# Gated linear attention and a cosine-gated layer on one Trainium2 core: where the weights' checks, the weights' halves and the log sums stand in the loop over groups

## The chip, the cores and the metric

The kernel runs on one core of one Trainium2 chip. The metric is device time in microseconds (us). Three runs of the kernel before gave 665.95, 669.12 and 670.2; their median is 669.12. One execution was recorded by the hardware profiler; every duration below is from it.

## The reference, cut to what matters

```python
# q, k, v, a_re, a_im: (B=4, H=8, S=768, D=48)
mag = np.sqrt(a_re * a_re + a_im * a_im)
scale = np.minimum(mag, 0.999) / (mag + 1e-06)
a_re_n, a_im_n = (a_re * scale, a_im * scale)
for t in range(S):
    ar, ai = (a_re_n[:, :, t, :, None], a_im_n[:, :, t, :, None])
    new_re = ar * S_re - ai * S_im
    new_im = ar * S_im + ai * S_re
    kv = np.einsum('bhd,bhe->bhde', k[:, :, t], v[:, :, t])
    S_re, S_im = (new_re + kv, new_im)
    y[:, :, t] = np.einsum('bhd,bhde->bhe', q[:, :, t], S_re)
x = y.transpose(0, 2, 1, 3).reshape(B * S, H * D)      # 3072 x 384
h = x @ w_in                                           # 384 x 2048
g = h * np.cos(h)
out = g @ w_out                                        # 2048 x 384
```

The state decays by a complex gate at each step; only its real part is read. The two weights arrive as 8-byte floats.

## The kernel before

**Chunks and groups.** The 768 steps of a batch are cut into chunks of 128 (24 chunks in all); two chunks make a group, so there are 12 groups, three to a batch. Within a chunk the recurrence is turned into products: a sum over time of the logs of the gates' magnitudes and a sum of their phases give, through exponentials and cosines, factors for the queries and keys; scores (`sc`, queries by keys, masked by VectorE into `atm`), value products (`yp`) and state sums (`sp`) follow on TensorE (PE). The group's result goes to memory as x and comes back turned as xT, two DMAs (L1066, L1075). Then come the group's hidden sums x @ w_in (`hp`, tiles jp = 0 to 7, each of 256 columns of w_in in two halves of 128 rows), the gate h*cos(h) (a sine with a shift of half pi on ScalarE (ACT), a check `junk`/`wide` on the size of h, a product on VectorE (DVE)), and the products with w_out, arranged as seven products of blocks of which the sums and differences (`s`, `t_s`, `t_a`, `gate` mixes) are made beforehand.

**Three-term tiles.** From group 3 on the tiles jp 4 and 5, from group 4 on also 6 and 7, are computed another way: the weight is cut into an upper part wh and a scaled rest wl (`halves`, L1099: three DVE instructions that make `cut`, wl and wx, then two ACT instructions that write wh and scale wl), and x into xh and xl (`x_halves`, L1116). PE then makes xh*wh + xl*wl (the straight part) and a cross sum `hb` from xx and wx.

**A software pipeline.** The loop `for n in range(2, NG)` (L1721) runs, for each n, attention of group n, the products of group n-1, the logs, keys and phases of group n+1 and the hidden sums of group n. `weave` (L1356) gives every list of steps a stretch of the interval 0 to 1 and writes the steps down in that order: attention and products fill the first half, `first(n)`, the eight hidden-sum tiles, stands from 0.56 to 1.0. A scheduler then orders each engine; `chain` fixes the order of PE, of ACT's table-based functions (`special`, L709, and `upper_half`, L726; the last of them is `tail["scalar"]`) and of SyncE's (SP's) DMAs; `behind(a, b)` puts a behind b on one engine. A last `weave` after the loop (L1738) does the products of group 11.

**Logs.** `log_steps` (L736 to L791) makes magnitude and angle of the gates of the next group; its last instruction is a Relu over `re` that adds up negative entries in `odd`. `upper_half` splits the logs into hi (ACT) and lo (DVE); `prods` (L1386) multiplies both by triangular ones on PE (`lgs`), and ACT takes the exponentials of it. The powers at a chunk's end leave through a small DMA called row (L843) and come back as `end` (L850). SP's queue carries, in the order of the program, row, the x and xT of the group, and at the group's end the turned keys and queries: two moves `moved<-tr` (L948), four `kT<-moved` (L951) and one `qT<-moved` (L953).

**Guards.** A check on the 8-byte weights rides along in the loop. `fetched` (L627) loads a piece of 768 KB by GpSimd's (POOL's) queue (L631) into a tile `raw`, which in the loop shares its one buffer (`tr`) with the turned keys and queries; `guard` (L647) takes the exponent from the upper words by a shift on DVE, and ACT's Relu of (897 - exponent) adds up what is too small, in place. `guarded` (L1425) first lets POOL wait for a named gate of group n-1. There are 16 pieces, two in each of the groups 4 to 11. POOL's wait stands at position 0.1; load and check of a group's first piece are written at 0.22, of its second at 0.93, the end of the hidden sums. The second load can go out when tr is free.

L691 is the line of every matmul, L680 that of nearly every DVE and ACT instruction that has no other helper, L711 that of the table functions, so what follows goes by tiles.

Of the kernel before, what the change touches and what calls it, by code (L numbers as in the profile page):

```python
# [11 lines left out]
F32 = mybir.dt.float32  # L12
# [475 lines left out]
def fast_path(ctx, tc, q, k, v, a_re, a_im, moe_w_in, moe_w_out, out, least, odd, wide,  # L488
# [46 lines left out]
    tail = {}  # L535
# [124 lines left out]
    least_e_b = scalar_tile(897.0, "least_e_b")  # L660
# [75 lines left out]
    def log_steps(g, i, n):  # L736
# [43 lines left out]
        if lower:  # L780
# [9 lines left out]
        scalar.activation(out=junk, in_=re, func=AF.Relu, scale=-1.0,  # L790
                          accum_out=odd[:, ds(next(odds), 1)])  # L791
# [307 lines left out]
    def halves(jp):  # L1099

        for name in "wl", "wx":
            if name not in right:
# [4 lines left out]
        vector.tensor_scalar(out=cut_.bitcast(U32), in0=w.bitcast(U32), scalar1=UPPER,  # L1107
                             scalar2=None, op0=ALU.bitwise_and)
# [4 lines left out]
        scalar.copy(out=w_in[jp], in_=cut_)  # L1113
        scalar.mul(out=wl, in_=wl.bitcast(F32), mul=SHIFT)

    def x_halves(g):  # L1116
# [14 lines left out]
        def lower():  # L1131
            behind(scalar.copy(out=x["xh"], in_=x["cut"]), x["square"])
# [3 lines left out]
            behind(low, x["product"])  # L1136

        def apart():
            behind(vector.scalar_tensor_tensor(
                out=x["xx"], in0=x["xl"].bitcast(F32), scalar=-SHIFT,  # L1140
                in1=x["cut"], op0=ALU.mult, op1=ALU.add), x["product"])
# [6 lines left out]
    def mm1_three(g, jp, ps):  # L1148
# [27 lines left out]
        for part in (straight, crossed) if "held" not in x else (crossed, straight):  # L1176
            part()
# [39 lines left out]
    def mm1(g, jp, last):  # L1217

        mm1_sums(g, jp)
        if three(g, jp):  # L1220
            cross_out(g, jp)
            if "held" in X[g]:
                mm1_gate(g, X[g]["held"])
# [4 lines left out]
        if last:  # L1228
# [3 lines left out]
            if "held" in X[g]:  # L1232
                mm1_gate(g, X[g]["held"])
# [191 lines left out]
    def guarded(g, count):  # L1425
# [3 lines left out]
        for _ in range(min(count, len(guards))):  # L1429
            yield lambda: guard(guards.pop(0), X[g + 1].get("product"))  # L1430
# [3 lines left out]
    per = -(-len(guards) // (NG - 4))  # L1434
# [399 lines left out]
```

## Time and profile before

| what | value |
|---|---|
| profiled execution, its own time | 670.13 us |
| its span in the trace | 668.2 us |
| PE matmul busy | 634.7 us, 95% |
| PE weight loads busy (beside matmuls) | 575.4 us, 86% |
| DVE busy | 528.7 us, 79% |
| ACT busy | 432.9 us, 65% |
| POOL busy | 31.2 us, 5% |
| chain that ended last | PE 70%, ACT 9%, DVE 8%, DMA 7% |

The span is the time from the first to the last recorded instruction; about 2 us of the execution lie around it. Busy shares are means over stages. A row of the timeline reads: start, duration, engine, line, operation, written tile<-read tiles, shape, count of instructions run together, and in brackets the idle time ahead of it and who ended it. For DMA issues the duration is the time on the issuing queue, not the transfer. A row of the windows reads: stretch and length, busy time (with instruction count) of PE, PE's weight loads, DVE, ACT and POOL, the granted clock of PE, the DMA engines' share and GB/s.

### The profile page before, as it was taken

The numbers are of one execution on the slowest core, as the hardware profiler recorded it, in microseconds if no ns is written. First come the engines' busy times: TensorE is split into PE (matmuls) and PEld (weight loads), VectorE is DVE, ScalarE is ACT, GpSimd is POOL, SyncE is SP. The second block draws the span as 40 slices with busy tenths as digits, with TensorE's granted clock in tenths as the row PEclk, the third lists the DMA queues.
The fourth block names the chain that finished last, engine by engine and source line by source line (L and its number), as shares of the span: only waits on it lengthen the run. The fifth ranks groups of instructions, "written<-read, shape, count | busy, mean of one in ns | idle before, by whom it ended". The sixth has DMA issues, their size and how long they took to land.

```text
span 668.2 us, 11342 instructions
## 1 busy us (share of the span) xinstructions
PE 634.7 (95%) x4279; PEld 575.4 (86%) x4279; DVE 528.7 (79%) x862; ACT 432.9 (65%) x787; POOL 31.2 (5%) x53
## 2 busy tenths in 40 slices
PE   8999989998899999989999999989989999999977
PEld 6888867766799899989989989989979999989977
DVE  6999989687598899788699799787779889873361
ACT  7898777372694794695695695596586586552440
POOL 4011100000000000000000000000000000000000
PEclk9999999999899999999999999998999999999999
DMA  9967855538417816936925926926844942544000
GB/s 237 258 189 170 250 142 152 120 71 218 89 26 165 237 25 137 256 82 127 270 78 119 270 75 132 272 71 123 231 108 84 278 110 52 173 88 142 24 2 29
DMA packets 232922, 94.93 MB, mean 142 GB/s; under 512 B 208701, under 2 KB 221246, under 8 KB 232858
## 3 DMA queue, kind: packets, MB, share of 16 engines
q1 hardware_dynamic: 225320, 68.51, 44.6%
q0 software_dynamic: 5824, 25.50, 11.4%
q8 instruction: 35, 0.57, 0.4%
q10 hardware_dynamic: 1714, 0.11, 0.2%
q14 instruction: 29, 0.24, 0.1%
HBM read 69.28 MB, written 24.81 MB: 141 GB/s over the span
## 4 chain that ended last, share of the span: by engine, by line
PE 70%; ACT 9%; DVE 8%; DMA 7%; issue 4%; SPq 1%; ACTq 0%; POOL 0%; POOLq 0%; DVEq 0%
PE hp L691 23%; PE op L691 14%; PE sum L691 14%; PE yp L691 5%; PE sc L691 4%; PE sp L691 3%; DMA qT<-moved 3%; PE phs L691 2%; PE hb L691 2%; ACT junk L680 2%; DVE hp L680 1%; ACT gate L711 1%; DMA xT<-x 1%; DVE gate L680 1%; PE lgs L691 1%
## 5 line engine op out<-in xcount | busy, mean ns | idle before, releaser
L691 PE MATMUL hp<-xT,w_in 128*128 128x256 f32 (+1 forms) x768 | 166.5, 376 | 7.1 <-DVE gate L680 5.1
L691 PEld LDWEIGHTS hp<-xT,w_in 128*128 128x128 f32 x768 | 143.0, 192 | 28.1 <-DVE gate L680 5.5
L711 ACT ACTIVATE gate<-hp,half_pi_b 128x512 f32<-128x512 f32 x96 | 65.9, 687 | 62.6 <-PE hp L691 45.7
L691 PE MATMUL op<-w_out,gate 128*128 128x192 f32 (+1 forms) x464 | 103.6, 373 | 1.2 <-DVE gate L680 1.2
L691 PEld LDWEIGHTS op<-w_out,gate 128*128 128x128 f32 x464 | 78.5, 190 | 18.7 <-issue 2.0
L680 DVE TENSOR_TENSOR gate<-hp,gate 128x512 f32<-128x512 f32 x62 | 42.5, 685 | 37.3 <-ACT junk L680 37.0
L680 ACT ACTIVATE ot<-sum 128x192 f32<-128x192 f32 x39 | 12.8, 328 | 72.3 <-PE sum L691 72.0
L691 PE MATMUL sc<-qT,kT 96*128 96x128 f32 x384 | 49.6, 277 | 10.5 <-DMA qT<-moved 7.8
L691 PEld LDWEIGHTS sc<-qT,kT 96*128 96x128 f32 x384 | 46.9, 192 | 13.4 <-issue 10.8
L680 ACT ACTIVATE junk<-hp 128x512 bf16<-128x512 f32 x96 | 56.7, 590 | 0.0
L691 PE MATMUL sum<-w_out,gate 128*128 128x192 f32 x304 | 54.6, 328 | 0.0
L691 PEld LDWEIGHTS sum<-w_out,gate 128*128 128x128 f32 x304 | 49.2, 190 | 0.0
L680 DVE SCALAR_TENSOR_TENSOR gate<-hp,gate 128x512 f32<-128x512 f32 x34 | 23.5, 691 | 25.9 <-ACT junk L680 25.9
L680 DVE TENSOR_TENSOR atm<-sc,causal 128x512 f32<-128x512 f32 x48 | 32.5, 684 | 8.6 <-PE sc L691 8.6
L691 PE MATMUL hp<-xh,wh 128*128 128x256 f32 x204 | 37.0, 290 | 0.0
L691 PE MATMUL hp<-xl,wl 128*128 128x256 f32 x204 | 35.2, 281 | 0.0
L691 PE MATMUL yp<-atm,v 128*48 128x128 f32 x352 | 34.2, 280 | 0.7 <-DVE atm L680 0.7
L691 PE MATMUL sum<-t_s,gate 128*128 128x192 f32 x160 | 31.7, 352 | 2.5 <-DVE gate L680 2.5
L680 DVE TENSOR_TENSOR gate<-gate 128x256 f32<-128x256 f32 x80 | 32.2, 419 | 1.9 <-PE op L691 1.3
L691 PEld LDWEIGHTS sum<-t_s,gate 128*128 128x128 f32 x160 | 27.4, 201 | 5.4 <-issue 4.4
L707 ACT ACT_TABLE_LOAD x24 | 30.8, 1283 | 1.2 <-PEq L1818 0.7
L691 PE MATMUL yp<-qT,state 96*48 96x128 f32 x304 | 30.4, 278 | 0.0
(163 smaller groups left out, 1240.0 us busy)
## 6 DMA issues: line engine op xcount, KB each, us to landing
moved<-tr SPq DMA_DIRECT2D x20, 768.0 KB
raw<-in_moe_w_in_dram POOLq DMA_DIRECT2D x16, 768.0 KB, 5.5
raw<-in_moe_w_out_dram POOLq DMA_DIRECT2D x16, 768.0 KB, 5.7
kT<-moved SPq DMA_DIRECT2D x40, 192.0 KB
qT<-moved SPq DMA_DIRECT2D x10, 768.0 KB
k<-in_k_dram SPq DMA_DIRECT2D x24, 192.0 KB
q<-in_q_dram SPq DMA_DIRECT2D x24, 192.0 KB
v<-in_v_dram SPq DMA_DIRECT2D x24, 192.0 KB
```

What stands on the lines that cost most here:

```text
L680: ins = getattr(self.engine, op)(**kw)
L691: chain(nc.tensor.matmul(out, **kw), "tensor")
L707: chain(nc.scalar.preload_act_table_set(table))
L711: chain(nc.scalar.activation(func=func, **kw))
```

## The change

1. `guard` no longer uses DVE: ACT takes the absolute value of the upper word, read as a 4-byte float and in place, and then the Relu against the float whose bits are 897 shifted left by 20. The absolute value stands behind the last chained ACT function. The checks stand in the groups 3 to 10, not 4 to 11, again two in each; load and check of the first piece are written at 0.26, of the second at 0.47, the wait of POOL stays at 0.1.
2. The Relu over `re` at the end of `log_steps` also stands behind the last chained function.
3. `prods`, the log sums, move from 0.25-0.27 to 0.2701-0.2735.
4. `halves`, the two conversions of weights in each of the groups 2 and 3, move from 0.7 and 0.76 to 0.82 and 0.93 and stand behind the latest gate product (DVE) and the latest gate square, the check `junk` (ACT), of their group.
5. In the last group (11) the hidden-sum tiles run in the order 0, 4, 1, 5, 2, 6, 7, 3, so plain and three-term tiles alternate; the halves of x stand earlier (0.53, 0.54 instead of 0.61, 0.65) and not behind gates; three of the four mixes of gates stand within the loop, not after it.
6. In a three-term tile the straight part comes first only for jp = 4 while one cross sum is out; a gate that waits for its cross sum is made in the next tile whatever its kind.

```diff
-    def guard(src, other=None):
+    def guard(src):
         _, e = fetched(src)
-        ins = vector.tensor_scalar(out=e, in0=e, scalar1=1, scalar2=21,
-                             op0=ALU.logical_shift_left, op1=ALU.logical_shift_right)
-        if other is not None:
-            behind(ins, other)
-        scalar.activation(out=e.bitcast(F32), in_=e, func=AF.Relu, scale=-1.0, bias=least_e_b,
+        bits = e.bitcast(F32)
+        behind(scalar.activation(out=bits, in_=bits, func=AF.Abs), tail["scalar"])
+        scalar.activation(out=bits, in_=bits, func=AF.Relu, scale=-1.0, bias=least_e_b,
                           accum_out=odd[:, ds(next(odds), 1)])
...
-    least_e_b = scalar_tile(897.0, "least_e_b")
+    least_e_b = scalar_tile(float(np.uint32(897 << 20).view(np.float32)), "least_e_b")
...
+        if g > PEG:
+            behind(checked, tail["scalar"])
...
-        vector.tensor_scalar(out=cut_.bitcast(U32), in0=w.bitcast(U32), scalar1=UPPER,
-                             scalar2=None, op0=ALU.bitwise_and)
+        behind(vector.tensor_scalar(out=cut_.bitcast(U32), in0=w.bitcast(U32), scalar1=UPPER,
+                                    scalar2=None, op0=ALU.bitwise_and), X[FROM[jp] - 1]["product"])
...
-        scalar.copy(out=w_in[jp], in_=cut_)
-        scalar.mul(out=wl, in_=wl.bitcast(F32), mul=SHIFT)
+        behind(scalar.copy(out=w_in[jp], in_=cut_), X[FROM[jp] - 1]["square"])
+        behind(scalar.mul(out=wl, in_=wl.bitcast(F32), mul=SHIFT), X[FROM[jp] - 1]["square"])
...
-        for part in (straight, crossed) if "held" not in x else (crossed, straight):
+        for part in (straight, crossed) if len(x["hb"]) == 1 and jp == THREE[0] else (crossed, straight):
...
-            if "held" in X[g]:
-                mm1_gate(g, X[g]["held"])
+        if "held" in X[g]:
+            mm1_gate(g, X[g].pop("held"))
+        if three(g, jp):
             X[g]["held"] = jp
...
+        if g == NG - 1:
+            order = 0, 4, 1, 5, 2, 6, 7, 3
...
-            yield lambda: guard(guards.pop(0), X[g + 1].get("product"))
+            yield lambda: guard(guards.pop(0))
...
-    per = -(-len(guards) // (NG - 4))
+    per = -(-len(guards) // (NG - 3))
...
-        guard_ = list(guarded(n - 1, per)) if n > 3 else []
+        guard_ = list(guarded(n - 1, per)) if n > 2 else []
...
-              (upper[2:] if plain else [], 0.0, 0.2), (products(n - 1, 0, 2 + (n < NG - 1)), 0.0, 0.36),
+              (upper[2:] if plain else [], 0.0, 0.2), (products(n - 1, 0, 2 + (n < NG - 1)), 0.0, 0.365),
...
-              (prods(n + 1), 0.25, 0.27), (second(n - 1, 1), 0.36, 0.5),
+              (prods(n + 1), 0.2701, 0.2735), (second(n - 1, 1), 0.36, 0.5),
...
-              (convert[0:1], 0.7, 0.7), (convert[1:2], 0.76, 0.76),
+              (convert[0:1], 0.82, 0.82), (convert[1:2], 0.93, 0.93),
...
-              (turned_keys[2:3], 0.56, 0.56), (turned_keys[3:4], 0.6, 0.6), (split[1:2], 0.61, 0.61),
-              (split[2:3], 0.65, 0.65), (last_quarter() if plain else [], 0.9, 1.0), (first(n), 0.56, 1.0),
-              (mixes(n, 0, 2 * (n < NG - 1)), 0.98 if convert else 0.92, 1.0), (guard_[0:1], 0.1, 0.1),
-              (guard_[1:2], 0.22, 0.22), (guard_[2:3], 0.93, 0.93))
+              (turned_keys[2:3], 0.56, 0.56), (turned_keys[3:4], 0.6, 0.6), (split[1:2], *[0.61 if n < NG - 1 else 0.53] * 2),
+              (split[2:3], *[0.65 if n < NG - 1 else 0.54] * 2), (last_quarter() if plain else [], 0.9, 1.0), (first(n), 0.56, 1.0),
+              (mixes(n, 0, 2 + (n == NG - 1)), 0.98 if convert else 0.92, 1.0 if n < NG - 1 else 0.97), (guard_[0:1], 0.1, 0.1),
+              (guard_[1:2], 0.26, 0.26), (guard_[2:3], 0.47, 0.47))
...
-    weave(([judged], 0.0, 0.0), (mixes(NG - 1, 0, 4), 0.01, 0.1),
+    weave(([judged], 0.0, 0.0), (mixes(NG - 1, 3, 4), 0.01, 0.1),
```

Three places of the order in which the engines run the program. The first is DVE in the second half of group 2, where the keys (ks) and queries (qs) of group 3 are turned into tr; `end` and `least` belong to the decay over a whole chunk, `cut`, wl and wx to the conversion of one weight tile, `gate<-hp,gate` is the product of h with its cosine. Before:

```order
L680 STREAM_TRANSPOSE tr<-ks 128x1536
L680 TENSOR_SCALAR end<-end 96x16
L680 STREAM_TRANSPOSE tr<-qs 128x1536
L680 SCALAR_TENSOR_TENSOR least<-end,least 96x16
L680 TENSOR_SCALAR cut<-w_in 128x768
L680 TENSOR_TENSOR wl<-w_in,cut 128x768
L680 SCALAR_TENSOR_TENSOR wx<-wl,cut 128x768
L680 TENSOR_TENSOR gate<-hp,gate 128x512
```

and now:

```order
L680 STREAM_TRANSPOSE tr<-ks 128x1536
L680 STREAM_TRANSPOSE tr<-qs 128x1536
L680 TENSOR_SCALAR end<-end 96x16
L680 SCALAR_TENSOR_TENSOR least<-end,least 96x16
L680 TENSOR_TENSOR gate<-hp,gate 128x512 x3
L680 TENSOR_TENSOR s<-gate 128x256
L680 TENSOR_TENSOR gate<-gate 128x2x128
```

The first conversion no longer stands between the turns and the first gate product; three gate products follow the turns.

The second place is ACT in the attention half of a typical later group: tan is the angle's and the log's work tile, hi the upper half of the logs, yT the copies of value products out of PSUM, `lg<-lgs` and `pair<-lgs` the exponentials of the log sums, raw the check. Before:

```order
L680 ACTIVATE re,odd<-re 128x768
L711 ACTIVATE tan<-tan 128x768
L732 ACTIVATE hi<-lg 128x768
L680 COPY yT<-yp 48x4x128 x2
L680 ACTIVATE raw,odd<-raw,least_e_b 128x768
L711 ACTIVATE lg<-lgs 128x384
L711 ACTIVATE pair<-lgs 128x384
```

and now:

```order
L711 ACTIVATE tan<-tan 128x768
L732 ACTIVATE hi<-lg 128x768
L680 ACTIVATE re,odd<-re 128x768
L680 ACTIVATE raw<-raw 128x768
L680 ACTIVATE raw,odd<-raw,least_e_b 128x768
L680 COPY yT<-yp 48x4x128 x2
L711 ACTIVATE lg<-lgs 128x384
L711 ACTIVATE pair<-lgs 128x384
```

The check on re stands behind hi; the guard is two instructions, ahead of the second pair of copies. The second guard of the group now follows `hi<-tan` (the phases' upper half) in the same way; before, it stood among the last gate sines of the hidden sums.

The third place is PE in the hidden sums of the last group, from their start. Before:

```order
L691 MATMUL hp<-xT,w_in 128x256 x24
L691 MATMUL hp<-xh,wh 128x256 x3
L691 MATMUL hp<-xl,wl 128x256 x3
L691 MATMUL hp<-xh,wh 128x256 x3
L691 MATMUL hp<-xl,wl 128x256 x3
L691 MATMUL hb<-xx,wx 128x256 x12
```

and now:

```order
L691 MATMUL hp<-xT,w_in 128x256 x6
L691 MATMUL hp<-xh,wh 128x256 x3
L691 MATMUL hp<-xl,wl 128x256 x3
L691 MATMUL hp<-xh,wh 128x256 x3
L691 MATMUL hp<-xl,wl 128x256 x3
L691 MATMUL hb<-xx,wx 128x256 x6
L691 MATMUL hp<-xT,w_in 128x256 x6
L691 MATMUL hb<-xx,wx 128x256 x6
```

The four plain tiles ran ahead of the four three-term tiles; now a plain tile (six matmuls of xT) stands between them, and the last six matmuls of the group are a plain tile's.

More of the change, by code (lines that the diff above doesn't have):

```diff
@@ L789, in log_steps @@
         junk = stage["pool"].tile([C, DM], BF16, tag="below", name="below", bufs=1) if n == 1 else re
-        scalar.activation(out=junk, in_=re, func=AF.Relu, scale=-1.0,
-                          accum_out=odd[:, ds(next(odds), 1)])
+        checked = scalar.activation(out=junk, in_=re, func=AF.Relu, scale=-1.0,
+                                    accum_out=odd[:, ds(next(odds), 1)])
+        if g > PEG:
+            behind(checked, tail["scalar"])
     def g_log(g, i, n):
@@ L1131, in lower @@
         def lower():
-            behind(scalar.copy(out=x["xh"], in_=x["cut"]), x["square"])
+            copied = scalar.copy(out=x["xh"], in_=x["cut"])
+            if g + 1 < NG:
+                behind(copied, x["square"])
             low = vector.tensor_tensor(out=x["xl"], in0=all_of(), in1=x["cut"], op=ALU.subtract)
@@ L1135, in lower @@
                 behind(low, X[g + 1]["qT turn"])
-            behind(low, x["product"])
+                behind(low, x["product"])
         def apart():
-            behind(vector.scalar_tensor_tensor(
+            apart_ = vector.scalar_tensor_tensor(
                 out=x["xx"], in0=x["xl"].bitcast(F32), scalar=-SHIFT,
-                in1=x["cut"], op0=ALU.mult, op1=ALU.add), x["product"])
+                in1=x["cut"], op0=ALU.mult, op1=ALU.add)
+            if g + 1 < NG:
+                behind(apart_, x["product"])
         return upper, lower, apart
@@ L1232, in mm1 @@
             if "held" in X[g]:
-                mm1_gate(g, X[g]["held"])
+                mm1_gate(g, X[g].pop("held"))
     def mm2(g, i, j0, nj):
```

## Prediction

> **What bounds the kernel now.** I read the page first, then the waits of TensorE (PE), then the chain that ended last, then the timeline of the places that these name. Here are the head of the page, its chain line, and the longest waits of PE (total us, times, longest).
>
> ```profile
> span 668.2 us, 11342 instructions
> PE 634.7 (95%) x4279; PEld 575.4 (86%) x4279; DVE 528.7 (79%) x862; ACT 432.9 (65%) x787; POOL 31.2 (5%) x53
> PE 70%; ACT 9%; DVE 8%; DMA 7%; issue 4%; SPq 1%; ACTq 0%; POOL 0%; POOLq 0%; DVEq 0%
> PE sc L691 <- DMA qT<-moved: 7.8, 6, 3.0
> PE hp L691 <- DVE gate L680: 5.1, 1, 5.1
> PE sum L691 <- DVE gate L680: 2.5, 1, 2.5
> PE sc L691 <- issue: 2.5, 2, 2.3
> PE lgs L691 <- DVE lo L680: 2.2, 3, 1.1
> ```
>
> PE is the bound: it is busy 95% of the span, so a gain can only come from the some 30 us in which it stands still and from places where it runs slowly. The waits are few: about ten us in front of the scores (sc, waiting for the turned queries qT), one of 5.1 in front of a hidden sum (hp), 2.5 in the tail (sum), 2.2 in front of the log sums (lgs). What they cost beyond themselves stands in the windows: the stretch and its length, busy time of PE, its weight loads, DVE, ACT and POOL, the granted clock of PE, DMA share and GB/s.
>
> ```profile
> 165.60:169.01 3.41, 0.11 (x1) 0.11 (x2) 1.26 (x3) 2.89 (x6) 0.00 (x0) 1.00 1.08 204
> 169.01:172.43 3.42, 3.42 (x9) 2.70 (x10) 2.94 (x4) 2.81 (x6) 0.00 (x0) 0.50 1.03 214
> 448.91:452.32 3.41, 1.88 (x18) 1.38 (x20) 3.41 (x6) 3.35 (x8) 0.00 (x0) 1.00 0.59 115
> 452.32:455.74 3.42, 3.42 (x28) 3.06 (x24) 3.42 (x7) 3.17 (x6) 0.00 (x0) 0.50 0.02 6
> 650.29:653.71 3.42, 3.42 (x13) 3.42 (x12) 1.27 (x4) 0.27 (x1) 0.00 (x0) 0.50 0.00 0
> ```
>
> Three stretches of 3.42 us ran at half clock (0.50), each behind one in which PE was busy 0.11 to 1.88 of 3.41 us. A stretch at half clock costs half of it, 1.7 us. So three waits are dearer than they look: the one at 169, the log sums at 450, the tail at 649.
>
> The Trainium skill, TensorE: Matmul & The Clock Gate (Part 1, what is actually happening), has free-running windows of 3.4 us and half clock after an idle window, and its closing table warns of gaps above some 3 us; the trace agrees on the length (3.42) but not on the condition, since 1.88 us of work in the window did not save the clock at 452. By the page's condition only the first of the three would count, and the sum below would gain about 3 us less.
>
> **The change part by part**, against the profiled execution's own 670.1 us (the median of the shown runs, 669.1, lies 1 us below it, their spread is 666.0 to 670.2).
>
> *Weights' halves later in group 2.* The timeline there:
>
> ```profile
> 155.78 7.98 PE L691 MATMUL hp<-xT,w_in 128*128 128x256 f32 x36
> 161.28 2.23 DVE L680 STREAM_TRANSPOSE tr<-qs 128x1536 f32<-128x1536 f32 x1
> 165.07 0.96 DVE L680 SCALAR_TENSOR_TENSOR wx<-wl,cut 128x768 fp32r<-128x768 f32 x1
> 166.12 0.84 ACT L680 ACTIVATE wl<-wl 128x768 fp32r<-128x768 f32 x1 [8.83 <-DVE wx L680]
> 168.16 0.69 DVE L680 TENSOR_TENSOR gate<-hp,gate 128x512 f32<-128x512 f32 x1 [2.12 <-ACT junk L680]
> 168.90 14.90 PE L691 MATMUL hp<-xT,w_in 128*128 128x256 f32 x60 [5.14 <-DVE gate L680]
> ```
>
> ScalarE (ACT) reached the scaling of wl first, and stood 8.83 us for VectorE's wx, which itself stood behind the key turns; the first gate sine was queued behind it. So three hidden sums filled PSUM and the fourth waited 5.14 us. Now the sines come first, and VectorE's first gate product follows the turn of qs (161.28 + 2.23, plus two 0.13 us instructions: 163.8). With 0.69 for the product PE can go on at 164.5 instead of 168.9, 0.75 us after it ran dry at 163.76. Saved: 4.4 of wait, 1.7 of clock. What is late next: the two conversions (three VectorE instructions of 0.55 to 0.96, two ACT of 0.84) fall into the end of group 2 and the start of group 3, where group 3's logs stand on ACT. I add for group 3: one wl and one wh behind the last gate (1.7), two guards that were not there before, of which one lies ahead of the arctan (2.0, priced next), a copy (0.6). That is 4.3 on ACT, against some 1.5 of slack: **+2.8** there (bounds 0 to +4.3).
>
> *Guards on ScalarE alone.* The groups of raw's instructions (count | busy us, mean ns):
>
> ```profile
> L680 ACT ACTIVATE raw<-raw,least_e_b 128x768 f32<-128x768 uint32 x16 | 16.0, 999 | 4.3 <-DVE raw L680 4.2
> L680 DVE TENSOR_SCALAR raw<-raw 128x768 uint32<-128x768 uint32 x16 | 8.9, 556 | 0.6 <-DMA raw<-in_moe_w_out_dram 0.6
> ```
>
> VectorE loses 16 x 0.56 us. ACT gains 16 absolute values; not in this trace, between the plain 128x768 activation (0.83) and the same strided words (1.00); I take 0.9. Nothing of this is on PE by itself. The place counts: the second guard's load. Without that load and with it:
>
> ```profile
> 161.34 2.52 SPq L948 DMA_DIRECT2D moved<-tr  x2
> 164.55 4.29 SPq L951 DMA_DIRECT2D kT<-moved  x4
> 168.95 1.00 SPq L953 DMA_DIRECT2D qT<-moved  x1
> 472.60 2.56 SPq L948 DMA_DIRECT2D moved<-tr  x2
> 475.84 8.64 SPq L951 DMA_DIRECT2D kT<-moved  x4
> 476.36 0.72 POOL L631 DMA_DIRECT2D raw<-in_moe_w_out_dram  x1 [32.88 <-ACT xh L680]
> 484.59 0.86 SPq L953 DMA_DIRECT2D qT<-moved  x1
> 491.38 1.13 PE L691 MATMUL sc<-qT,kT 96*128 96x128 f32 x8 [3.04 <-DMA qT<-moved]
> ```
>
> The raw tile shares its buffer with the turned keys (tr), so the second load went out (476.36) the moment the keys had left it, beside the moves of kT and qT. Four issues of kT then took 8.64 us on SP's queue instead of 4.29, qT was issued 12.0 us after the first move instead of 7.6, and PE stood 3.04 us for it. Now the second load goes out when the first guard's Relu is done, in the middle of attention, and lands (7.9 us at the worst here) before the next keys. That gives qT back 2 to 4 us in each group; the scores lacked 0.3 to 3.0. Both sc rows above, 10.3 us, should go; I take **-9.5**. If the load were not the cause: 0.
>
> *Log sums behind value products.* The lgs matmuls move behind the second chunk's value products (1.8 us of PE work), so lo is there: -2.2 of that row and 0.5 for hi, **-2.7**, and **-1.7** for the clock at 452. Bounds 0 to -4.4.
>
> *What this triggers.* With the score wait gone PE reaches the group's second half earlier, and there the inputs xT must be there. A typical group:
>
> ```profile
> 385.54 0.69 ACT L711 ACTIVATE gate<-hp,half_pi_b 128x512 f32<-128x512 f32 x1 [0.94 <-DVE hp L680]
> 386.13 1.00 ACT L680 ACTIVATE raw<-raw,least_e_b 128x768 f32<-128x768 uint32 x1
> 404.05 0.84 ACT L711 ACTIVATE tan<-tan 128x768 f32<-128x768 f32 x1
> 408.67 0.24 SPq L843 DMA_DIRECT2D row<-lg  x1
> 412.21 0.38 SPq L1075 DMA_DIRECT2D xT<-x  x1
> 416.99 10.52 PE L691 MATMUL hp<-xT,w_in 128*128 128x256 f32 x48
> 612.99 0.38 SPq L1075 DMA_DIRECT2D xT<-x  x1
> 617.49 0.56 DVE L680 TENSOR_SCALAR cut<-xT 128x768 uint32<-128x768 uint32 x1 [4.13 <-DMA xT<-x]
> ```
>
> From the end of the hidden sums (385.2) to the arctan ACT has no pause, and the arctan leads through VectorE to the row's DMA (408.67); the stores and loads of x stand behind row on SP's queue, xT at 412.21, and hp took its place at 416.99 without a wait. xT needs at most 4.5 us (612.99 to 617.49). Now on ACT from 385.2 to the arctan: minus the late guard (1.2), plus the absolute value (0.9), plus half of the second pair of yT copies (0.6), with the exponentials behind later value products: row comes at about +23.9 us instead of +23.5. And +3.5 to xT, +3.4 to +4.5 to its landing: 30.8 to 31.9 after the hidden sums, where PE needs 29.4 to 31 with its score wait gone. So a part of the gain returns as a wait for xT: 0.1 to 2.4 a group, about 0.9 in seven groups, **+6.5** (bounds 0 to +14), and with some chance of one more stretch at half clock, **+0.6**.
>
> *Last group.*
>
> ```profile
> 639.46 2.82 PE L691 MATMUL sum<-w_out,gate 128*128 128x192 f32 x16
> 649.10 4.30 PE L691 MATMUL sum<-t_s,gate 128*128 128x192 f32 x16 [2.48 <-DVE gate L680]
> ```
>
> Plain and split tiles alternate and the last tile is a plain one: its sine, square and product (0.69 + 0.59 + 0.2 + 0.69 and the queue ahead of it) end 2.9 us after the hidden sums instead of 6.2. The mixes of the first three pairs are done before, so the s products start 6.8 us behind the hidden sums instead of 9.6: **-2.8**; and the half clock at 650 goes if the wait inside a window stays under 1.5: **-1.3**.
>
> Sum: -4.4 - 1.7 + 2.8 - 9.5 - 2.7 - 1.7 + 6.5 + 0.6 - 2.8 - 1.3 = -14.2, so **656.0 us**.
>
> **The rivals.**
>
> (1) The ACT chain is longer than counted: absolute values at 1.0, the copies waiting for value products, row 1.5 us later in seven groups. For it: ACT has no pause from 385.5 to 404, so each added piece moves row. Against: one guard leaves that stretch. 656 + 7 x 1.5 = 666.5, no change that can be told.
>
> (2) The moves of kT are slow by themselves, and only half of the score waits goes: 656 + 5 = 661. For it: in the short group without a load PE came late, so nobody saw when qT was there. Against: 4.29 against 8.64.
>
> (3) The second load holds up x instead of kT. It leaves about 15.6 us behind the hidden sums; row, x and xT leave from 23.9 on. Once it lands later than 8.3 us after its issue, every xT comes later, and at the 4.35 us that it cost the four kT issues, in six groups, the time is 656 + 6 x 4.35 = 682, slower; it decides from 2.4 us a group on. Against it: the worst landing of sixteen is 7.9 us.
>
> The Trainium skill, DMA: Bandwidth & Descriptors (issuing engines are not separate DMA queues), says that queues of all issuers run on the same 16 engines and interleave, so a load moved in time still costs whoever is beside it; by that rule (3) is the case to fear, and the slower kT issues beside raw agree with it.
>
> (4) xT is there in time (it lands sooner than 3.4): the +6.5, +0.6 and part of the +2.8 fall away: 656 - 9 = 647.
>
> **How the numbers follow.** Forecast 0.55, (1) 0.16, (2) 0.13, (3) 0.05, (4) 0.11. One per cent is 6.7 us, about what a measurement can tell here from no change: below 662.4 is faster. That holds the forecast, (2) and (4) but for their upper edges, 0.78; (1) and these edges make 0.17; (3) makes 0.05. The range reaches from (4) to (1): 647 to 667.
>
> **What would show it.** Right: no 5 us wait before a hidden sum near 169; the wait of sc for qT under 2 us in all, SP's four kT issues near 4.3 us; lgs without waits, one half-clock stretch at most; new waits of hp for xT of about a microsecond, in the groups where a batch ends the longest; in the tail one short wait. Wrong: sc waits as before although raw is loaded in attention (then raw was not the cause); hp waits above 2 us in most groups (rival 1 or 3: row late, or xT late behind row); a new stall of ACT at the second absolute value, whose load is late.

## The result and the profile after

| | before | changed |
|---|---|---|
| median of the runs, us | 668.65 (665.95 to 670.2, four runs) | 659.99 (657.27 to 662.06, four runs) |
| ratio, 95% interval | 1 | 0.987 (0.982 to 0.992) |
| profiled execution, us | 670.13 | 662.06 |
| its span, us | 668.2 | 660.3 |
| busy PE, DVE, ACT, us | 634.7, 528.7, 432.9 | 632.5, 522.4, 446.5 |

The forecast was 656.0 in a range of 647 to 667. The kernel became faster by 1.3%, by 8.7 us where 14 were forecast. The head of the changed kernel's page and its chain line:

```profile
span 660.3 us, 11335 instructions
PE 632.5 (96%) x4279; PEld 573.7 (87%) x4279; DVE 522.4 (79%) x846; ACT 446.5 (68%) x803; POOL 30.8 (5%) x53
PE 60%; ACT 19%; DVE 8%; DMA 7%; issue 4%; SPq 1%; ACTq 0%; DVEq 0%
```

PE is still the bound, but ScalarE's share of the chain went from 9% to 19%: that chain now decides several times when PE may go on. The waits of PE (total us, times, longest):

```profile
PE hp L691 <- DMA xT<-x: 8.6, 6, 3.4
PE hp L691 <- ACT raw L680: 2.4, 1, 2.4
PE sum L691 <- DVE gate L680: 1.7, 4, 0.6
PE hp L691 <- DVE ks L680: 1.2, 1, 1.2
PE hp L691 <- DVE qs L680: 1.0, 1, 1.0
PE sc L691 <- issue: 0.3, 1, 0.3
```

The waits of sc for qT (7.8 + 2.5 us) are gone but for 0.3, so are the 5.1 us of hp behind a gate and those of lgs for lo. In their place stands one thing nearly alone: hp waits for xT, 8.6 us in six places, and two more of the same sort, in groups 6 and 8, that the table books under DVE (ks, qs): xT went out 3.5 and 3.8 us ahead of their ends, as in the other groups. The 2.4 of `raw` lie at 88.6, ahead of group 2. From the trace, the time at which the scores of a group start, and the waits for xT just ahead of the hidden sums:

| stretch | before | changed | difference | forecast |
|---|---|---|---|---|
| start to scores and products of group 2 | 128.4 | 130.9 | +2.4 | 0 |
| from there to the hidden sums of group 2 | 27.3 | 31.3 | +4.0 | 0 |
| hidden sums of group 2, to the scores of group 3 | 27.9 | 22.3 | -5.6 | -6.1 |
| group 3, scores to scores | 49.8 | 52.0 | +2.2 | +2.8 and its share of the xT waits (0.9) |
| groups 4 to 10 | 359.7 | 352.4 | -7.3 | -7.7 |
| group 11 to the end | 75.1 | 71.5 | -3.6 | -4.1 |

The columns sum to -7.9 us, the difference of the spans. All terms but two came within 1.6 us, and their misses cancel; the two stand at the top, and make up 6.4 us, the miss. The first is no work of the change: PE waited 2.43 us at 88.6 where it had waited 1.94 in the profile before, and the next stretch ran at half clock. The first kernel of the experiments, which runs in the same order up to there, did not wait at this place and came to the scores of group 2 at 127.5, against 128.4 before and 130.9 in the changed kernel. The second is the subject of the experiments. In groups 4 to 10 the gain lies in 4, 8 and 10 (-1.4, -5.0, -2.3); 5, 6, 7 and 9 became 0.1 to 0.7 us longer, so there the wait only moved from the scores to the hidden sums. The windows of both places (stretch, length, busy PE, its weight loads, DVE, ACT, POOL, granted clock, DMA share, GB/s):

```profile
86.60:90.01 3.41, 1.38 (x7) 1.26 (x8) 2.26 (x3) 2.83 (x5) 0.00 (x0) 1.00 0.74 242
90.01:93.42 3.41, 3.41 (x10) 2.88 (x9) 3.38 (x5) 0.00 (x0) 0.00 (x0) 0.50 0.58 110
158.27:161.68 3.41, 0.45 (x2) 0.00 (x0) 3.29 (x4) 1.80 (x3) 0.00 (x0) 1.00 0.91 203
161.68:165.09 3.41, 2.93 (x7) 2.39 (x8) 3.41 (x3) 0.00 (x0) 0.00 (x0) 0.50 1.11 223
```

Three stretches at half clock in which PE worked (169, 452, 650) became two. One is 0.26% of the mean clock of a run and 1.7 us; the four runs of the changed kernel have mean clocks of 0.997, 0.994, 0.995 and 0.992 at 657.3, 659.9, 660.1 and 662.1 us, so part of what differs between them is probably how many such stretches each meets; the profiled one, the slowest of the four, is the only one whose stretches are seen.

The Trainium skill, TensorE: Matmul & The Clock Gate (what is actually happening), asks for an idle window ahead of half clock; PE was busy for 1.38 us of the window at 86.6, so the measurement again differs from it, as at 452 before.

**Where group 2 lost 4 us.** ScalarE there, before:

```profile
141.13 0.49 ACT L711 ACTIVATE lg<-lgs 128x384 f32<-128x384 f32 x1 [0.26 <-PE lgs L691]
142.79 1.28 ACT L707 ACT_TABLE_LOAD   x1
144.12 0.84 ACT L711 ACTIVATE tan<-tan 128x768 f32<-128x768 f32 x1
144.87 0.56 ACT L680 COPY yT<-yp 48x512 f32<-48x512 f32 x1
```

and in the changed kernel:

```profile
142.84 0.49 ACT L680 ACTIVATE ot<-op 128x384 f32<-128x384 f32 x1
146.50 1.17 ACT L680 COPY yT<-yp 48x512 f32<-48x512 f32 x2 [3.17 <-PE yp L691]
147.68 0.49 ACT L711 ACTIVATE lg<-lgs 128x384 f32<-128x384 f32 x1
149.34 1.28 ACT L707 ACT_TABLE_LOAD   x1
150.63 0.84 ACT L711 ACTIVATE tan<-tan 128x768 f32<-128x768 f32 x1
```

The exponentials of the log sums (`lg<-lgs`) once ran ahead of the second chunk's copies of yT; now they stand behind them, and those wait 3.17 us for the value products yp. So the arctan comes at 150.6, 6.5 us later than before, of which 2.4 are from the start. SP's queue and PE behind it:

```profile
154.78 0.24 SPq L845 DMA_DIRECT2D row<-lg  x1
155.08 0.80 SPq L1068 DMA_DIRECT2D x<-yT  x2
158.35 0.38 SPq L1077 DMA_DIRECT2D xT<-x  x1
```

```profile
162.16 1.22 PE L691 MATMUL hp<-xT,w_in 128*128 128x256 f32 x2 [3.44 <-DMA xT<-x]
```

row goes out at 154.78 (148.25 before), x behind it, xT when x has landed, and PE stands 3.44 us.

### The profile page after: what moved, and what is told of

Read it like the earlier page. It is cut to its first block, busy times and chain, and to the rows that moved or that the text cites. A ratio compares the mean times of both kernels' runs of the same rounds, so it can differ in the third digit from the quotient of the medians.

```text
span 660.3 us, 11335 instructions
## 1 busy us (share of the span) xinstructions
PE 632.5 (96%) x4279; PEld 573.7 (87%) x4279; DVE 522.4 (79%) x846; ACT 446.5 (68%) x803; POOL 30.8 (5%) x53
## 4 chain that ended last, share of the span: by engine, by line
PE 60%; ACT 19%; DVE 8%; DMA 7%; issue 4%; SPq 1%; ACTq 0%; DVEq 0%
PE hp L691 29%; PE op L691 10%; PE sum L691 6%; PE sc L691 4%; DMA xT<-x 3%; PE yp L691 3%; PE hb L691 2%; ACT tan L711 2%; PE sp L691 2%; DMA x<-yT 2%; ACT raw L680 2%; ACT rs L711 2%; ACT L707 2%; ACT yT L680 2%; ACT pair L711 2%
## 5 line engine op out<-in xcount | busy, mean ns | idle before, releaser
L691 PE MATMUL hp<-xT,w_in 128*128 128x256 f32 (+1 forms) x768 | 168.4, 378 | 13.1 <-DMA xT<-x 8.6
L680 DVE SCALAR_TENSOR_TENSOR gate<-hp,gate 128x512 f32<-128x512 f32 x34 | 23.5, 690 | 22.8 <-ACT junk L680 22.8
L680 ACT COPY yT<-yp 48x512 f32<-48x512 f32 x44 | 25.4, 577 | 14.0 <-PE yp L691 13.3
L691 PE MATMUL sum<-t_s,gate 128*128 128x192 f32 x160 | 29.8, 332 | 1.4 <-DVE gate L680 1.2
L691 PEld LDWEIGHTS hp<-xh,wh 128*128 128x128 f32 x204 | 29.7, 189 | 0.5
```

The costliest lines, as they stand in the source:

```text
L680: ins = getattr(self.engine, op)(**kw)
L691: chain(nc.tensor.matmul(out, **kw), "tensor")
```

## The experiments

Twelve kernels ran. The theory: PE's time between the hidden sums of two groups is set by a row of steps, ScalarE's functions up to the arctan, VectorE's last factor, row, x, xT; the change lengthens it by 4 us in group 2, and a little in the others. Rivals: xT is late by DMA traffic, or the sc waits went for another reason than the load's place.

### The late log sums of group 2

```diff
-              (prods(n + 1), 0.2701, 0.2735)
+              (prods(n + 1), *((0.25, 0.27) if n == 2 else (0.2701, 0.2735)))
```

> The changed kernel with the log sums of one pass of the loop, n = 2, back at 0.25-0.27; every later group keeps them late. Theory: in group 2 the late log sums leave ScalarE idle until the second chunk's value products are there, row goes out 4 us later, and PE waits 3.4 us for xT and then runs a stretch at half clock; both go: 654 to 656 us, with the wait at 162 us under 1.2 us and everything from group 3 on as in the changed kernel. Rival: something else in group 2 holds xT (the conversions moved out of it, the table load): the wait stays above 2.5 us and the time at 659 to 661.

Measured: 655.52 us, ratio 0.981 (0.976 to 0.985); the wait in question:

```profile
155.75 9.55 PE L691 MATMUL hp<-xT,w_in 128*128 128x256 f32 x43 [1.07 <-DMA xT<-x]
```

1.07 us instead of 3.44, and the profiled run shows a mean clock of 1.000: no stretch at half clock. From the scores of group 2 to those of group 3 it takes 49.0 us instead of 53.6, so 4.5 us are this edit's, with the stretch; the profiled span is 7.7 shorter because 3.3 us more fell away ahead of group 2, at the place near 88. The six runs reach from 653.5 to 661.3 and the interval overlaps that of the changed kernel (0.982 to 0.992), so the trace shows the cause better than the medians do. It is the theory's number, and the fastest of the kernels here that keep all the checks of the weights.

### All log sums back

```diff
-              (upper[2:] if plain else [], 0.0, 0.2), (products(n - 1, 0, 2 + (n < NG - 1)), 0.0, 0.365),
+              (upper[2:] if plain else [], 0.0, 0.2), (products(n - 1, 0, 2 + (n < NG - 1)), 0.0, 0.36),
...
-              (prods(n + 1), 0.2701, 0.2735)
+              (prods(n + 1), 0.25, 0.27)
```

> The changed kernel with the log sums back at 0.25-0.27 (and the end of the first products at 0.36), nothing else undone. Theory: the later log sums put the second pair of yT copies ahead of the exponentials on ScalarE, so row and behind it on SP's queue x and xT go out later. Undone, the wait of hp for xT in group 2 (3.4 us) goes, those of groups 3 to 9 (7.3 in all) fall to under 3, and the waits of lgs come back (2 to 3 us, perhaps one stretch at half clock): 653 to 656 us. Rival: the lgs waits are worth more than the xT waits, as the diff has it: xT waits stay above 6 us in all and the time goes to 662 to 665.

Measured: 664.31 us, 0.991 (0.988 to 0.994). Half of the theory fell. In group 2 the wait went (0.93), but in the later groups most of those for xT stayed (6.6 us by the table of waits) and 4.5 us of lgs came back:

```profile
PE lgs L691 <- DVE lo L680: 3.4, 5, 1.2
PE lgs L691 <- ACT hi L732: 1.1, 4, 0.4
```

Against the kernel with only group 2 undone, the late log sums of groups 3 to 11 are worth 664.3 - 655.5 = 8.8 us by the medians, twice the 4.4 of the forecast: 4.5 are the lgs waits and 1.7 a stretch at half clock at 191; the rest is spread over small waits for gates and scores and over longer products, mostly in groups 3, 5, 8 and 10. Why xT stayed late, in group 5 of this kernel (SP's queue, POOL's, ScalarE):

```profile
304.92 0.24 SPq L845 DMA_DIRECT2D row<-lg  x1
305.26 0.81 SPq L1068 DMA_DIRECT2D x<-yT  x2
312.16 0.38 SPq L1077 DMA_DIRECT2D xT<-x  x1
```

```profile
304.29 0.75 POOL L631 DMA_DIRECT2D raw<-in_moe_w_in_dram  x1 [14.59 <-ACT raw L680]
```

```profile
311.16 0.90 ACT L680 ACTIVATE raw<-raw 128x768 f32<-128x768 f32 x1 [2.42 <-DMA raw<-in_moe_w_in_dram]
```

row left early (304.92), x at 305.26, but xT only 6.9 us after x instead of 3.1 to 4.2: the second load of raw had gone out at 304.29 and landed at about 311. In the changed kernel that load lies at 303.3 to 309.3 in this group, ahead of x (311.36), which is followed by xT after 3.2. So the same step is held by two things, ScalarE's chain when it is long, and the second load when the chain is short. That is the mechanism of rival (3) of the prediction, in another kernel; in groups 3, 5, 8 and 10 of this one xT followed x after 5.7 to 6.9 us, though PE waited over half a microsecond for it in group 5 alone (1.47). In groups 6, 7 and 9, with waits of 1.4 to 1.8, xT followed x after 3.5 to 3.7, and row left 23.5 to 23.8 us behind the hidden sums, much as in the changed kernel (23.7 to 24.0), although the arctan came 1.2 to 2.2 us earlier: in group 6 VectorE does two more instructions (a mix of gates and a factor, 0.42 + 0.95 us) ahead of row's last factor. So neither the load nor ScalarE alone explains these three. The Trainium skill, DMA: Bandwidth & Descriptors (issuing engines are not separate DMA queues), says that all issuers' transfers interleave on the same engines; the rows of group 5 agree.

### The weights' halves, alone and with the log sums of group 2

```diff
-              (convert[0:1], 0.82, 0.82), (convert[1:2], 0.93, 0.93),
+              (convert[0:1], 0.7, 0.7), (convert[1:2], 0.76, 0.76),
...
-        behind(scalar.copy(out=w_in[jp], in_=cut_), X[FROM[jp] - 1]["square"])
+        scalar.copy(out=w_in[jp], in_=cut_)
...
```

> The changed kernel with the conversions of weights back at 0.7 and 0.76 and not behind gates. Theory: VectorE again makes the first weight's halves ahead of the first gate product, and the wait of hp for it in group 2 (5.1 us, one stretch at half clock) comes back, and in group 3 likewise if its turns are as late: 664 to 667 us. Rival: the wait for xT that now stands ahead of these hidden sums gives VectorE the time, and the wait for the gate stays under 2 us: 659 to 662.

Measured: 661.26 us, 0.989 (0.985 to 0.994), not told apart from the changed kernel; the rival was right:

```profile
160.20 12.20 PE L691 MATMUL hp<-xT,w_in 128*128 128x256 f32 x48 [3.47 <-DMA xT<-x]
172.72 2.64 PE L691 MATMUL hp<-xT,w_in 128*128 128x256 f32 x11 [0.32 <-DVE gate L680]
```

With 3.47 us of waiting for xT ahead of the hidden sums VectorE had the time, and the wait for the gate was 0.32. With the log sums of group 2 back as well:

> The kernel with the log sums of group 2 back, and the weights' conversions back at 0.7 and 0.76 as well. Theory: the late log sums of the changed kernel put a wait of 3.4 us for xT ahead of the hidden sums of group 2, and this wait covers the conversions, so that undoing them alone cost little (661.3 against 660.0); without that wait they cost what the prediction charged, a wait for the first gate of 4 to 5 us at 167 us and a stretch at half clock: 660 to 662 us against 655.5. Rival: the conversions no longer cost anything because other instructions of the change cleared VectorE: wait under 1.5 us, 655 to 657.

Measured: 660.17 us, 0.985 (0.980 to 0.990), against 655.52 without this edit; the intervals overlap, but the trace tells them apart:

```profile
155.22 8.04 PE L691 MATMUL hp<-xT,w_in 128*128 128x256 f32 x36 [0.69 <-DMA xT<-x]
167.40 2.93 PE L691 MATMUL hp<-xT,w_in 128*128 128x256 f32 x6 [4.15 <-DVE gate L680]
```

Now the wait for the gate is 4.15 us, and its stretch runs at half clock. From the scores of group 2 to those of group 3 it takes 54.5 us instead of 49.0. So the 4.4 + 1.7 that the prediction charged for this edit are near its price when xT is in time. As the kernel was changed, a second edit put a wait of nearly that size in front of the same sums, and the two share one wait.

### The place of the second load

```diff
-              (guard_[1:2], 0.26, 0.26), (guard_[2:3], 0.47, 0.47))
+              (guard_[1:2], 0.22, 0.22), (guard_[2:3], 0.93, 0.93))
```

> The changed kernel with load and check of the two pieces of a group back at 0.22 and 0.93, the checks still on ScalarE alone. Theory: the second load, which then goes out when the keys have left tr, runs beside the four kT moves: their issues take 8 us on SP's queue instead of 4 to 5, the waits of sc come back to 7 to 10 us in all, those of hp for xT fall under 4: 664 to 668 us. Rival: the sc waits are gone because PE now comes later by its wait for xT, and the loads' place does not matter: sc waits under 2 us, 658 to 661.

Measured: 677.22 us, 1.012 (1.003 to 1.021). The sc waits are back, 11.1 us in seven places:

```profile
PE sc L691 <- DMA qT<-moved: 9.6, 6, 2.8
PE sc L691 <- issue: 1.5, 1, 1.5
```

SP's queue at the end of group 8:

```profile
483.74 6.91 SPq L953 DMA_DIRECT2D kT<-moved  x4
490.76 0.78 SPq L955 DMA_DIRECT2D qT<-moved  x1
```

```profile
484.25 0.72 POOL L631 DMA_DIRECT2D raw<-in_moe_w_out_dram  x1 [33.12 <-DVE gate L680]
```

```profile
497.95 1.13 PE L691 MATMUL sc<-qT,kT 96*128 96x128 f32 x8 [2.83 <-DMA qT<-moved]
```

With the load at 484.25 beside them four kT issues take 6.91 us; in the changed kernel, without it, 3.90 (group 7):

```profile
427.23 3.90 SPq L953 DMA_DIRECT2D kT<-moved  x4
431.25 0.95 SPq L955 DMA_DIRECT2D qT<-moved  x1
```

In all groups 3 to 10 of this version such a load stands beside the four issues, which take 6.2 to 8.1 us; in the changed kernel those without one take 3.8 to 4.0 us, 4.7 and 5.3 in groups 9 and 10. That shows the cause behind the term of -9.5, and rival (2), slow moves of their own, falls. What was not expected: the xT waits did not shrink (10.0 us), so both kinds are paid; with four stretches at half clock instead of two this version is 17 us slower than the changed kernel, and slower than the kernel before.

### ScalarE's chain: guards that only load, guards with a VectorE mask, none

```diff
-        bits = e.bitcast(F32)
-        behind(scalar.activation(out=bits, in_=bits, func=AF.Abs), tail["scalar"])
-        scalar.activation(out=bits, in_=bits, func=AF.Relu, scale=-1.0, bias=least_e_b,
+        bits = e.bitcast(F32)[:, 0:1, 0:1]
+        scalar.activation(out=bits, in_=bits, func=AF.Relu, scale=-1.0, bias=least_e_b[:, 0:1],
```

> The changed kernel with guards that load all of each piece but check one word of each row (absolute value and most of the Relu left out). Theory: two ScalarE instructions ahead of the arctan (1.9 us) hold row, and so xT; without them row goes out about 1.9 us earlier after the hidden sums and the waits of hp for xT in groups 3 to 9 (7.3 us in all) fall under 1.5; group 2, which has no guard, keeps its 3.4: about 653 us. Rival: the loads themselves, beside x and xT on the DMA engines, hold xT: the waits stay at 6 us or more and the time at 658 to 661.

Measured: 2053.75 us, which says nothing here: without the absolute value negative weights count in `odd`, and the program ran its second, general path behind the first. The first path's trace stands for itself. The waits for xT of groups 3 to 9 are 2.6 us instead of 7.3, group 2 keeps 3.6, and the loads are all there. So not the loads but the instructions hold xT in the changed kernel; there, in groups 2 to 9, no load of raw runs between the issues of x and xT. In the one group in which a load still ran beside the moves, qT was issued 12.2 us after the first move and sc waited 2.9, against 7.5 to 8.7 and none elsewhere in the same trace.

```diff
-        _, e = fetched(src)
...
+        return
```

> The kernel with the log sums of group 2 back, and without the guards in the loop: their loads, absolute values and Relus are left out, so the weights are not checked. Theory: the guards of the changed kernel cost through ScalarE's chain, 1.9 us ahead of the arctan; without them the waits of hp for xT in groups 3 to 9 fall under 2.5 us in all, and nothing else waits: 647 to 650 us. Rival: the chain is long without them too (yT copies and exponentials behind the later value products), the waits stay above 6 us: 653 to 656.

Measured: 648.59 us, 0.967 (0.963 to 0.971), 6.9 under the kernel with the guards (655.52). Its waits:

```profile
PE hp L687 <- DMA xT<-x: 4.7, 7, 1.0
```

4.1 of the 4.7 lie in groups 3 to 9, more than the 2.5 expected, and 8.8 with guards. row leaves up to 1.1 us earlier in these groups, not the 1.9 that was expected. So some 4.7 of the 6.9 us go through xT; where the rest lies was not followed.

```diff
-        behind(scalar.activation(out=bits, in_=bits, func=AF.Abs), tail["scalar"])
-        scalar.activation(out=bits, in_=bits, func=AF.Relu, scale=-1.0, bias=least_e_b,
-                          accum_out=odd[:, ds(next(odds), 1)])
+        vector.tensor_scalar(out=e, in0=e, scalar1=0x7FFFFFFF, scalar2=None, op0=ALU.bitwise_and)
+        behind(scalar.activation(out=bits, in_=bits, func=AF.Relu, scale=-1.0, bias=least_e_b,
+                                 accum_out=odd[:, ds(next(odds), 1)]), tail["scalar"])
```

> The kernel with the log sums of group 2 back, and the absolute value of the guards made by VectorE (a bit mask on the same words, same places) instead of ScalarE. Theory: ScalarE's chain to the arctan sets row, and row sets xT; one instruction of 0.93 us less ahead of the arctan brings row 0.9 us nearer to the hidden sums' end, and the waits of hp for xT in groups 3 to 9 (9 us with that of group 2) fall by 4 to 6 us: 650 to 652. Rival: VectorE is as full there, and its instruction delays the mixes or the factors by as much, or the second load now runs beside x: waits of 8 us or more, 655 to 659.

Measured: 659.43 us, 0.984 (0.979 to 0.989): no gain, 0.4 above the rival's 655 to 659. The Relu now waits for VectorE and stands between the table load and the arctan, and xT waits come to 7.7 us in groups 3 to 9; the longest, 2.45, cost a stretch at half clock as well. A shorter busy time on an engine isn't a shorter chain.

### x ahead of row on the queue

```diff
-        yield lambda: (f_x(g), f_xt(g))
+        def out_():
+            f_x(g)
+            f_xt(g)
+            if g + 1 < NG:
+                row_out(g + 1, 0, G, Late)
+                row_back(g + 1, 0, G, Late)
+        yield out_
...
```

Late puts a DMA behind xT on SP's queue; the loads of k, q, v and the stores use it too.

> The changed kernel with another order on SP's queue: x and xT ahead of row, and row, end, the loads of k, q, v and the stores of the output behind xT. Theory: x stands ready some 4 to 7 us before row does, and xT is late only because it is queued behind row; with xT ahead the waits of hp (10.7 us in all) fall under 2 and the stretch at half clock in group 2 goes: 648 to 652 us. Rival: x is late by its own copies and by the landing of its store, or the loads beside it hold it: waits of 6 us or more, 657 to 661; a second rival: row, now 1 to 3 us later, holds up the state or the turned keys, and the scores wait again: sc waits above 4 us.

Measured: 685.32 us, 1.022 (1.016 to 1.029). In group 2 PE still waited 4.46 us for xT. In the later groups xT did go out earlier, 24.8 us after the group's scores instead of 28.3 in group 6, and from group 3 on PE waits for it nowhere, though PE now also comes later. The scheduler also reordered VectorE. Of the same group:

```profile
343.45 0.96 DVE L680 SCALAR_TENSOR_TENSOR pair<-re,pair 128x768 f32<-128x768 f32 x1 [0.87 <-ACT pair L711]
345.15 0.96 DVE L680 TENSOR_TENSOR lg<-lg,rs 128x768 f32<-128x768 f32 x1
346.02 0.68 DVE L680 TENSOR_TENSOR atm<-sc,causal 128x512 f32<-128x512 f32 x1
```

```profile
346.76 0.64 PE L691 MATMUL yp<-atm,v 128*48 128x128 f32 x8 [3.39 <-DVE atm L680]
```

The mask of the second chunk's scores (atm) stands behind three log instructions, and PE waits 3.39 us for it; in all:

```profile
PE yp L691 <- DVE atm L680: 24.1, 15, 3.4
```

So the step was shown, but not what it is worth: the edit changed two things. The second try gives row and end to GpSimd's queue:

```diff
-            row_out(g, i, n, nc.sync)
-            row_back(g, i, n, nc.sync)
+            row_out(g, i, n, nc.sync if g <= PEG else nc.gpsimd)
+            row_back(g, i, n, nc.sync if g <= PEG else nc.gpsimd)
...
```

> As the kernel with the log sums of group 2 back, and row with its return end on GpSimd's queue instead of SP's, so that x no longer stands behind row. Theory: x goes out some 2 to 3 us earlier after the hidden sums; xT then stands only behind the loads of k, goes out 1 to 1.5 us earlier, and the waits of hp for xT in groups 3 to 9 (7.3 us in all) fall under 3: 649 to 652 us. Rival: x leaves no sooner or lands later beside the second load of raw, or end comes so late over GpSimd's queue that the state or the scores wait: 655 us or more.

Measured: 665.79 us, 0.992 (0.989 to 0.996), 10 us slower than without the edit:

```profile
157.85 0.17 DVE L680 TENSOR_SCALAR end<-end 96x16 f32<-96x16 f32 x1 [4.09 <-DMA end<-row]
165.84 1.87 DVE L680 TENSOR_TENSOR gate<-hp,gate 128x512 f32<-128x512 f32 x3
```

VectorE stands 4.09 us for end, with the turns and the first gate products queued behind it, and PE 3.56 us for the gate. But the edit changed two things again: in the kernel without it VectorE reads end behind the turns, at 162.13, and does not wait; here the scheduler put it ahead of the factors of the keys, and end was there at 157.85. So this trace doesn't show that GpSimd's queue is too slow for end, only what it costs in that place. x, now earlier, meets the end of the second load in groups 3 to 8, and the loads of k still stand ahead of xT, which in groups 3 to 9 follows 3.7 to 6.9 us after x; PE's waits for xT come to 9.6 us.

### The last group

```diff
-        if g == NG - 1:
-            order = 0, 4, 1, 5, 2, 6, 7, 3
...
-              (mixes(n, 0, 2 + (n == NG - 1)), 0.98 if convert else 0.92, 1.0 if n < NG - 1 else 0.97)
+              (mixes(n, 0, 2 * (n < NG - 1)), 0.98 if convert else 0.92, 1.0)
```

> The changed kernel with the last group's tiles in the old order (plain ones first), the halves of x at 0.61 and 0.65 and all four mixes after the loop. Theory: the last three-term gate and the mixes behind it come too late again, PE waits 3 to 4 us in the tail (for op and sum), with a stretch at half clock: 663 to 665 us. Rival: the tail's order is worth nothing, since the mixes hide behind the first products: 659 to 661.

Measured: 665.63 us, 0.993 (0.990 to 0.995), 5.6 above the changed kernel by the medians; from the scores of group 11 to the end 76.0 us instead of 71.5, so 4.5 are shown to be the tail's.

```profile
640.20 0.92 PE L691 MATMUL op<-w_out,gate 128*128 128x192 f32 x4 [0.41 <-DVE gate L680]
643.59 4.52 PE L691 MATMUL sum<-t_s,gate 128*128 128x192 f32 x16 [2.48 <-DVE gate L680]
```

The waits of the tail are back (2.48 as before), with a stretch at half clock; in the changed kernel one of 0.44 is left.

### Guards where the chain is not needed

```diff
-        guard_ = list(guarded(n - 1, per)) if n > 2 else []
+        some = {8: 2, 9: 2, 10: 2, NG - 1: 5}.get(n, 1 if n > 2 else 0)
...
```

> The kernel with the log sums of group 2 back, all sixteen guards kept but dealt out otherwise: one in each of the groups 3 to 7, at 0.47, behind the arctan; two in each of the groups 8 to 10; five in group 11, which makes no keys, no logs and no row, and whose xT stands ready 10 us ahead of the hidden sums. Theory: what the guards cost is their place ahead of the arctan, and without one there the waits of hp for xT in groups 3 to 7 fall as without guards (from 6.8 to about 3.6 us): 650 to 652.5 us, below both kernels and below the one with the log sums of group 2 back. Rival: the five in group 11 stand ahead of yT, of the copies of sums and of the first gates on ScalarE while their loads land, and PE waits there for what it won before: 655 us or more.

Measured: 663.76 us, 0.992 (0.990 to 0.995). The first half held: the xT waits of groups 3 to 7 fall to 3.0 us from 6.8, and the scores of group 11 start at 577.2, 5.9 us ahead of the kernel with guards in pairs. The second half was the rival's:

```profile
608.89 0.90 ACT L680 ACTIVATE raw<-raw 128x768 f32<-128x768 f32 x1 [5.62 <-DMA raw<-in_moe_w_out_dram]
609.69 0.30 ACT L680 ACTIVATE ot<-sum 128x192 f32<-128x192 f32 x1
```

```profile
610.05 4.39 PE L691 MATMUL sum<-w_out,gate 128*128 128x192 f32 x16 [7.57 <-ACT ot L680]
```

The third load of group 11 took until 608.8, ScalarE stood for it with the copy of a sum (`ot<-sum`) queued behind, and PE waited 7.57 us for that copy. A place between (fewer guards in group 11) was not tried.

## Why the prediction was right, and where it missed

**Sign and size.** Right in sign and within the range; 8.7 us of 14. The changed kernel without one of its edits at one place runs at 655.5, near the 656.0 of the sum, and in part by luck: between the profiles of that kernel and the kernel before, groups 4 to 10 gave 5.2 us where 7.7 were forecast, the last group 5.5 where 4.1 were.

**Halves in group 2 (-4.4 - 1.7).** The wait of 5.14 went, as said. The step that failed is "what is late next" of the log sums, not of the halves: the prediction put exponentials and copies of yT in another order "in seven groups", counted 0.6 us for it, and did not look at group 2, where ScalarE has no guard, is there early, and so waits 3.17 us for yp. PE waited 3.44 us for xT in front of the very sums whose wait had been taken away. Undone alone the halves cost nothing that can be told; with xT in time, 4.7 us.

**Group 3 (+2.8).** Measured +2.2, of which 1.47 are a wait for xT; with its share of the new waits 3.7 were forecast.

**Scores (-9.5).** Measured -10.0; the cause shown by moving the load back.

**Log sums (-2.7 - 1.7).** The waits went and so did the stretch at 452. In the changed kernel the edit is worth more: taken back in groups 3 to 11 it costs 8.8 us, of which 6.2 are lgs waits and a stretch at half clock, and the waits for xT do not fall in return. The prediction priced only the wait that it saw.

**New waits for xT (+6.5 + 0.6).** In groups 3 to 9: 1.47, 0.65, 1.20, 1.20, 0.92, 0.96, 0.86, together 7.3, and no stretch at half clock among them. row goes out 24.0 us after the hidden sums' end in the group that the prediction showed, where 23.9 was forecast and 23.5 was before; PE goes on 3.5 to 4.1 us after xT's issue where 3.4 to 4.5 was; the absolute value takes 0.91 to 0.96 us where 0.9 was. So the mechanism was right too: in groups 5 to 9 row leaves after 23.3 to 24.0 us, 23.3 to 24.5 before, and PE waits mainly because it comes earlier, without its wait for the scores. In groups 3 and 4 row did become later (20.9 to 24.3, 23.2 to 24.9). That rival (1) names the copies that wait for value products was right in kind, but in the wrong group.

**Tail (-2.8 - 1.3).** Measured -3.6. To PE's last matmul it is -5.5; the last store of the output then took 6.0 us instead of 4.2, a stretch that lies between 4.1 and 6.1 us in the profiles of the other kernels.

## What to carry to other kernels

Where two edits each remove or make a wait in front of the same work, their prices don't add: work out for each group which of the two ends last once both are in. A step that is late by one chain in one variant can be late by a transfer in the next, so name both before making the chain shorter. And when the scheduler orders the engines, an edit to one queue can move another engine's work: compare every engine's order before its time is believed.

## What the runs showed of the hardware

The load of xT was issued 3.1 to 4.6 us after the store of x in the kernels that kept the order of SP's queue, where no load of 768 KB ran between the two issues, and 5.5 to 6.9 where one ran on for 4.6 us or more behind the first. Four kT issues took 3.7 to 5.7 us with no such load beside them and 6.2 to 8.6 where one went out up to 1.4 us behind the first. The same load took 4.4 to 8.1 us, and once 10.6, the third load of group 11 in the kernel with five guards there, with no other issue seen beside it but that of xT just before; why stays open. PE dropped to half clock behind windows with 0 to 2.0 us of work out of 3.41 (2.01 ahead of 191 in the kernel with all log sums back); a single wait of 1.90 us was followed by it in the kernel with the old last group, at 213, and one of 1.88 was not in the kernel with the log sums of group 2 back, at 362.
